# Norm products on maxima over four tokens, scalings and sums of the first layer moved between engines, and later reads of the raw weights

## The chip, the cores and the metric

The kernel runs on one core of a Trainium2 chip. A core has a matrix engine (TensorE, in the profile PE, with its weight loads as PEld), a vector engine (VectorE, DVE), a scalar engine (ScalarE, ACT), a general engine (GpSimd, POOL) and a queue engine (SyncE, SP). The engines run their own instruction streams and wait for each other through semaphores. SP and POOL issue most of the DMAs, each in its own order. The metric is the device time of one execution in microseconds (us).

## The reference

Two identical layers run over a sequence of 2048 tokens of width 448. Each layer is attention with 16 heads of 28 features, and then a gated unit of width 1792, both on normalised input and added to the residual:

```
x = x + A(_layernorm(x), wqkv, wo)
x = x + B(_layernorm(x), w_gate, w_up, w_down)
# twice, with the same weights

A:  scores = q @ k.T * Dh ** -0.5;  p = softmax(scores);  o = (p @ v) @ wo
B:  h = sigmoid(x @ w_gate) * (x @ w_up);  h @ w_down
```

All inputs and the output are float32.

## The kernel before

**Precision.** Float32 products are made of float16 matmuls: an operand is scaled by a power of two and split into a high and a low half, and three products (high by high, high by low, low by high) are summed in PSUM. The powers of two come from sums of squares of the weights, so each weight matrix is read once raw and measured before it can be split. The class `Measure` does that for a part of the later weights (`wo`, `w_down`, the first columns of `w_gate` and `w_up`) during the projection of layer 0: `read` loads one raw tile (`wo` and three of the four tiles of `w_down` on SP's queue, the rest on POOL's), `add` sums its squares into a column of `sums`, on DVE (L958), and for the second half of the gate and up tile on ACT (L965). The class `Prepare` does the rest during the attention.

**The projection.** The 2048 tokens are four blocks of 512, each of four tiles of 128. `project` works in this order: query and key products of block 0, values of block 0, the same of block 1, then the query and key products of blocks 2 and 3, then the values of both. `qk(b, ...)` makes seven tiles of 128 features by 512 tokens, each of eleven matmuls (L564), into four PSUM banks that go round (`evac[0] % 4`, shared with the value products). After each tile ACT writes the high half (L756), DVE the low half (L757), ACT the squares (L759), DVE the maximum of the two halves of the tokens (L761), and SP writes the halves to `qk_scr` in DRAM (L764). Then the entry of the list `fill` that belongs to the tile is called: work for other blocks is put there, and so stands at that place in every engine's stream. `vals(b, ...)` makes four tiles of values (L586 to L591); its entries of `after` stand ahead of the tile's evacuation on ACT (L793).

**Norm products.** The squares, after the maximum, are multiplied by an indicator of heads (`norm_products`, L735 and L738): four matmuls for the queries and four for the keys of a block, three tiles behind. Their maxima over the columns (L775) give the largest norm of a query and of a key for each head, with which a bound on every score is formed (`guard_of_norms`). The bound is subtracted ahead of the exponential; if it is above `GUARD_LIMIT / 2`, a slow branch finds the true maxima (`worst_of_heads`, `true_maxima`).

**A block's operands.** A later block is normalised and turned so that features lie on partitions. `norm` takes mean and variance on DVE (L287, L288) and the reciprocal root on POOL (L291, L293). Block 1 of layer 0 is scaled (`scale`, L320) and turned by PE into banks 6 and 7, two feature groups at a time (`turned`, L508); ACT and DVE split it from there. The other blocks go through DRAM: scaled and transposed in squares of 32 by DVE (`squares`, L337), stored by four DMAs (`store`, L349), gathered by two (`gather`, L357, L359), and split by ACT and DVE (`ready`, L218, L219). In the gated part of the kernel another form of the same step is in use: `norm_two` adds two POOL operations for an offset (L302, L304), `lift` scales on ACT (L308), `square` transposes on DVE (L316).

**Order.** The schedule is written by hand: each engine runs its instructions in the order in which the program names them. Buffers come from two pools of slots (`big` and `qrt`), in which the slot that has been free longest is given out first.

Of the kernel before, what the change touches and what calls it, by code (L numbers as in the profile page):

```python
# [42 lines left out]
UNIT = 32768.0  # L43
VC = 32
SLACK = 1.0201
GUARD_LIMIT = 56.0


POWER_OF_2 = (1.0000001192092896, -0.6931469440460205, 0.24022120237350464,
# [69 lines left out]
def interleaved_layers(ctx: ExitStack, tc: tile.TileContext, x_in, wqkv, wo, w_gate, w_up,  # L119
# [143 lines left out]
    class Block:  # L263
# [52 lines left out]
            nc.vector.transpose(self.xs[:, :, j, :], v)  # L316
            qrt.put(v)

        def scale(self, j):
            nc.vector.tensor_scalar(self.xn[:, j, :], x[:, self.b * TB + j, :],  # L320
                                    self.mv[:, j, 0:1], self.rs[:, j:j + 1],
                                    op0=ALU.subtract, op1=ALU.mult)

        def parts(self):
            self.all = big.get("xhl", [P, 7, W], F16)
# [274 lines left out]
    class WeightsQKV:  # L600
# [111 lines left out]
    def project(layer, wq, begun):  # L712
# [12 lines left out]
        def qk(b, blk, fill, before):  # L725
            pn = [bank(4 + 2 * (b % 2), "qnorm"), bank(5 + 2 * (b % 2), "knorm")]
            late = deque()

            def rows_of_heads(i):

                return ind[:, i:i + P // H, :].rearrange("p a h -> p (a h)")

            def norm_products(i, sq):
                if i <= 3:
                    nc.tensor.matmul(pn[0][:, 0:W // 2], rows_of_heads(i), sq[:, 0:W // 2],  # L735
                                     start=(i == 0), stop=(i == 3))
                if i >= 3:
                    nc.tensor.matmul(pn[1][:, 0:W // 2], rows_of_heads(1 + i), sq[:, 0:W // 2],  # L738
                                     start=(i == 3), stop=(i == 6))
                qrt.put(sq)  # L740

            for i in range(7):
                pm = bank(evac[0] % 4, "qkp")
                evac[0] += 1
                c = slice(i * P, (i + 1) * P)
                by_features(pm, blk, lambda kt: wq.qk[0][:, kt, c],
                            lambda kt: wq.qk[1][:, kt, c], i if layer == 0 and b == 0 else None)
                if layer == 0 and b == 0:
                    along[i]()
                if before and i in (1, 2):  # L750
                    before(i == 2)
                if len(late) == 3:
                    late.popleft()()
                hl = qrt.get("qkhl", [P, 2, W], F16)
                sq = qrt.get("sq", [P, W], BF16)
                nc.scalar.activation(hl[:, 0, :], pm, AF.Copy, scale=PS)  # L756
                nc.vector.scalar_tensor_tensor(hl[:, 1, :], pm, PS, hl[:, 0, :], op0=ALU.mult,  # L757
                                               op1=ALU.subtract)
                nc.scalar.activation(sq, hl[:, 0, :], AF.Square)  # L759

                nc.vector.tensor_tensor(sq[:, 0:W // 2], sq[:, 0:W // 2], sq[:, W // 2:W],  # L761
                                        op=ALU.max)
                n = slice(b * W, (b + 1) * W)
                nc.sync.dma_start(qk_scr[c, :, n], hl)  # L764
                qrt.put(hl)
                late.append(lambda i=i, sq=sq: norm_products(i, sq))
                if i < len(fill) and fill[i]:
                    fill[i]()

            def finish(whole=True):  # L770

                while len(late) > (0 if whole else 1):
                    late.popleft()()
                for i in range(2 if whole else 0):
                    nc.vector.tensor_reduce(peaks[:, i, b:b + 1], pn[i][0:H, 0:W // 2], axis=AX.X,  # L775
                                            op=ALU.max)
            return finish

# [42 lines left out]
        sq = lambda b, *js: lambda: blks[b].squares(js)  # L821
        b1, b2, b3 = blks[1:]
        if layer == 0:
            def scaled():
                b1.xn = big.get("xn", [P, TB, D])
                for j in range(TB):
                    b1.scale(j)

            def turned(kts):
                b1.turn_banks(6, kts)  # L830
                for j in range(TB):
                    b1.turn(j)
                b1.turned_high()
                b1.turned_low()

            fill = [idle, idle, lambda: b1.norm([0, 1]), lambda: b1.norm([2, 3]), idle, scaled]
            tell = Measure()
            along_values = {0: lambda: (b1.parts(), turned([0, 1]), tell.read(2)),
                            1: lambda: (turned([2, 3]), big.put(b1.xn), tell.read(2)),
                            2: lambda: (fin(), b2.norm(), tell.read()),  # L840
                            3: lambda: (b2.squares(), b2.store(), tell.read())}
        else:
            ones_of_values()
            fill = [idle, lambda: b1.ready(0, 1), lambda: b1.ready(2, 3), b2.norm,
                    lambda: b2.squares([0, 1]), sq(2, 2, 3), b2.store]
            along_values = {0: b3.norm, 1: sq(3, 0, 1), 2: lambda: (fin(), b2.gather()),
                            3: sq(3, 2, 3)}
        fin = qk(0, blks[0], fill, None)
        vals(0, blks[0], along_values)
        if layer == 0:  # L850
            fill = [b2.gather, b3.norm, sq(3, 0, 1), sq(3, 2, 3), idle,
                    lambda: b2.ready(0, 1), lambda: (b2.ready(2, 3), b3.store())]
        else:
            fill = [idle, lambda: b2.ready(0, 1), lambda: b2.ready(2, 3), b3.store]
        fin = qk(1, b1, fill, None)
        vals(1, b1, {0: b3.gather, 2 if layer == 0 else 1: fin})
        add = tell.add if layer == 0 else idle
        fin = qk(2, b2, [idle, lambda: b3.ready(0, 1), lambda: b3.ready(2, 3), idle, add, add,
                         add], None)
        fin = qk(3, blks[3], [add, add, add], fin)  # L860
        if layer > 0:
            big.put(*wq.qk)
# [62 lines left out]
    class Measure:  # L925
# [27 lines left out]
        def add(self):  # L953
            kind, t, n = self.rows.popleft()
            m, n = {"o": (3, n), "d": (6, n), "gu": (4, 1024)}[kind]
            v = t[:, 0:n]
            junk = big.get("junk", [P, 2048], BF16)
            nc.vector.tensor_tensor_reduce(junk[:, 0:n], v, v, 1.0, sums[:, m:m + 1],  # L958
                                           op0=ALU.mult, op1=ALU.add,
                                           accum_out=self.part[:, 0:1])  # L960
# [945 lines left out]
```

## Time and profile before

| | |
|---|---|
| runs shown | 1895.25 us median of 3 (1894.69 to 1895.59) |
| profiled execution, first to last instruction (span) | 1893.0 us |
| median of the runs less that span | 2.25 us |
| projection of layer 0, from the first product to the first scores | 13.0 to 118.4 us |
| projection of layer 1 | 953.5 to 1055.3 us |
| granted TensorE clock | 1.000 |

The page gives the profiled execution by its span; what lies around it is seen only as the difference to the runs. The rows that follow are of three kinds. A row of the timeline has the start in us, the duration in us, the engine, the line of the kernel, the operation, the tiles (out, then in), the shape and the number of instructions merged; what ended the engine's idle time ahead of it stands in brackets. A row of the groups has the count, then the busy time in us and the mean of one in ns, then the idle time ahead. A row of the waits has who waited for whom, the total in us, how often, and the longest.

### The profile page before, as it was taken

Reading aid. Unit: us, or ns where it says so; the run is one execution under the profiler, and the core shown is the slowest. Engines: PE = TensorE matmul, PEld = TensorE weight load, DVE = VectorE, ACT = ScalarE, POOL = GpSimd, SP = SyncE. Lnnn points to the kernel's source line nnn. Section 1 sums busy time; section 2 is a strip of 40 time slices with the busy share of each in tenths; the row PEclk is TensorE's granted clock in tenths of the full one; section 3 lists DMA queues with packets and bytes.
Section 4 is the critical chain, followed back from the end, with each engine's and each line's share of the span. In section 5 each row is a group of like instructions: output and inputs, shape, how many; then the busy total and the mean of one; then the engine's idle time right before and its main releaser. Section 6 shows DMA issues by size and latency. Waiting matters only on the chain. (4 is left out here: it accounts for less than half of the span.)

```text
span 1893.0 us, 56282 instructions
## 1 busy us (share of the span) xinstructions
PE 1886.5 (100%) x24254; PEld 1323.1 (70%) x24254; DVE 1430.7 (76%) x2835; ACT 1382.7 (73%) x1772; POOL 231.5 (12%) x453
## 2 busy tenths in 40 slices
PE   9999999999999999999999999999999999999999
PEld 4455555555556799999954556667666567999998
DVE  7758989898976688787564487787778676887664
ACT  5569999999993566555345799999999745565541
POOL 3023112222101111111100000000000020121110
PEclk9999999999999999999999999999999999999999
DMA  7676454334323566646734322122120245666553
GB/s 247 194 212 166 132 137 128 107 119 129 103 88 121 192 205 235 231 181 238 251 96 134 90 52 47 32 52 52 31 48 24 67 160 174 218 251 223 208 208 142
DMA packets 110882, 270.86 MB, mean 143 GB/s; under 512 B 13214, under 2 KB 67838, under 8 KB 110496
## 3 DMA queue, kind: packets, MB, share of 16 engines
q0 software_dynamic: 31776, 158.51, 23.4%
q1 hardware_dynamic: 78288, 108.20, 20.3%
q8 instruction: 192, 3.15, 0.7%
q10 hardware_dynamic: 560, 0.46, 0.1%
q14 instruction: 66, 0.54, 0.1%
HBM read 207.88 MB, written 50.85 MB: 137 GB/s over the span
## 5 line engine op out<-in xcount | busy, mean ns | idle before, releaser
L1222 ACT ACTIVATE prob_s<-sc 128x1536 f32<-128x1536 f32 (+1 forms) x657 | 887.9, 1487 | 6.6 <-PE sc L1207 5.9
L1258 PE MATMUL acc<-prob_s,val_s 128*32 128x256 f32 (+3 forms) x7700 | 569.9, 383 | 0.0
L1207 PE MATMUL sc<-qp_s 114*32 114x512 f16 x7868 | 553.2, 379 | 0.0
L579 PEld LDWEIGHTS <-gu_s 128*128 128x128 f16 x4368 | 426.9, 98 | 46.8 <-issue 0.4
L1207 PEld LDWEIGHTS <-qp_s 114*32 114x32 f16 x8192 | 272.7, 95 | 203.4 <-issue 88.3
L1258 PEld LDWEIGHTS acc<-prob_s,val_s 128*32 128x32 f32 x7700 | 272.3, 110 | 142.9 <-issue 13.6
L579 PE MATMUL chain<-xwide_s,gu_s 128*128 128x256 f16 x2016 | 247.5, 273 | 0.0
L1552 PE MATMUL dnp<-dn_s,hparts_s 128*128 128x224 f16 x2016 | 225.2, 259 | 0.0
L1552 PEld LDWEIGHTS <-hparts_s 128*128 128x128 f16 x2016 | 194.0, 98 | 4.4
L1238 DVE SCALAR_TENSOR_TENSOR power_q<-power_q,expo_q 128x512 f32<-128x512 f32 x243 | 168.2, 692 | 8.3
L1625 ACT COPY one_q<-chain 128x256 f32<-128x256 f32 x224 | 82.4, 371 | 121.4 <-PE chain L579 120.8
L1641 DVE TENSOR_TENSOR one_q<-side,one_q 128x512 f32<-128x512 f32 x112 | 72.2, 686 | 101.8 <-PE side L579 101.5
L579 PE MATMUL side<-xshort_s,gu_s 128*128 128x256 f16 x1120 | 140.5, 273 | 0.0
L564 PE MATMUL qkp<-xhl_s,wqk_s 128*128 128x512 f16 x616 | 138.1, 379 | 0.7 <-ACT wqk_s L231 0.2
L564 PEld LDWEIGHTS <-wqk_s 128*128 128x128 f16 x616 | 60.1, 98 | 69.8 <-ACT wqk_s L231 1.1
L1437 POOL DMA_DIRECT2D gu_s<-gu_parts x104 | 56.0, 538 | 430.5 <-PE side L579 424.5
L1287 DVE STREAM_TRANSPOSE oturned_q<-acc 128x512 f32<-128x512 f32 x32 | 22.9, 716 | 97.1 <-PE acc L1258 96.9
L1258 PE MATMUL acc<-power_q,val_s 128*32 128x256 f32 (+3 forms) x300 | 94.2, 396 | 0.0
L579 PE MATMUL side<-xwide_s,gu_s 128*128 128x256 f16 x672 | 91.6, 273 | 0.0
L1505 ACT CAST hparts_s<-hsums_q 128x256 f16<-128x256 f32 (+1 forms) x136 | 65.0, 494 | 30.2 <-DVE hsums_q L1517 20.2
L756 ACT ACTIVATE qkhl_q<-qkp 128x512 f16<-128x512 f32 x56 | 33.2, 593 | 71.9 <-PE qkp L564 68.3
L1652 ACT ACTIVATE one_q<-one_q 128x512 f32<-128x512 f32 x56 | 35.2, 629 | 64.3 <-DVE one_q L1641 64.3
(218 smaller groups left out, 2318.0 us busy)
## 6 DMA issues: line engine op xcount, KB each, us to landing
gu_s<-gu_parts POOLq DMA_DIRECT2D x104, 800.0 KB, 6.0
dn_s<-dn_parts POOLq DMA_DIRECT2D x42, 784.0 KB, 7.8
qp_s<-qk_scr SPq DMA_DIRECT2D x96, 224.0 KB
qk_scr<-qkhl_q SPq DMA_DIRECT2D x56, 256.0 KB
gu_parts<-pack_s POOLq DMA_DIRECT2D x14, 800.0 KB, 3.8
xt_scr<-xs_s SPq DMA_DIRECT2D x48, 224.0 KB
xraw_s<-xt_scr SPq DMA_DIRECT2D x12, 768.0 KB
qp_s<-qk_scr SPq DMA_DIRECT2D x64, 112.0 KB
```

The source lines that it names most:

```text
L564: nc.tensor.matmul(pm, w, x, start=(i == 0), stop=(i == len(terms) - 1))
L579: nc.tensor.matmul(pm, a, x, start=(first and i == 0), stop=(i == len(terms) - 1), skip_group_check=True)
L1207: nc.tensor.matmul(ps[32 * j:32 * j + 32, :], hd.k[:, keys], hd.q[:, qb * W:(qb + 1) * W], start=True, stop=True, tile_position=(0, 32 * j))
L1222: nc.scalar.activation(prob[:, 0:n, :], ps[:, 0:n, :], AF.Exp, scale=exp_scale)
L1238: nc.vector.scalar_tensor_tensor(p, p, c[k], y, op0=ALU.add, op1=ALU.mult)
L1258: nc.tensor.matmul(acc[qb * VC:(qb + 1) * VC, s], v[:, kc % TB, h, :], probs[c * NB + qb][:, s], start=(kc == 0 and a == 0), stop=(kc == N ...
L1437: queue.dma_start(self.gu[-1][m], gu_parts[p, m])
L1505: nc.scalar.copy(to[:, :, 0], a)
L1552: nc.tensor.matmul(pm, a[:, x, t], w[:, p, y], start=(begin and n == 0 and (j == 0 or alone)), stop=(n == 2), skip_group_check=True)
L1625: nc.scalar.copy(to, pm)
L1641: nc.vector.tensor_tensor(one[m], side[m], one[m], op=ALU.add)
L1652: nc.scalar.activation(out, v, AF.Sigmoid, scale=gate_scale)
```

## The change

- The maximum over two tokens is followed by a second one over the halves of its result, so that each column stands for four tokens. The norm products and the reductions behind them take 128 columns instead of 256, in both layers. `GUARD_LIMIT` goes from 56 to 72.
- Layer 0, block 1: tiles 0 and 1 are scaled on POOL, right after their statistics and ahead of those of tiles 2 and 3 in POOL's order; tiles 2 and 3 on DVE, where all four were.
- Layer 0, blocks 2 and 3: `norm_two`, `lift` and `square` take the place of `norm` and `squares`, so the scaling is ACT's. Block 2's gather moves from the entry of block 1's first tile to the second, where block 3's statistics stay, and block 3's store moves from the seventh tile to the fourth.
- The six raw tiles are read one at a time from block 1's third tile to block 2's third tile; they were read along block 0's values.
- The first and third tile of `w_down` are squared and summed on ACT, with a small addition on DVE, instead of on DVE.

```diff
-GUARD_LIMIT = 56.0
+GUARD_LIMIT = 72.0
...
-        def scale(self, j):
-            nc.vector.tensor_scalar(self.xn[:, j, :], x[:, self.b * TB + j, :],
-                                    self.mv[:, j, 0:1], self.rs[:, j:j + 1],
-                                    op0=ALU.subtract, op1=ALU.mult)
+        def scale(self, j, engine=nc.vector):
+            engine.tensor_scalar(self.xn[:, j, :], x[:, self.b * TB + j, :],
+                                 self.mv[:, j, 0:1], self.rs[:, j:j + 1],
+                                 op0=ALU.subtract, op1=ALU.mult)
...
-                    nc.tensor.matmul(pn[0][:, 0:W // 2], rows_of_heads(i), sq[:, 0:W // 2],
+                    nc.tensor.matmul(pn[0][:, 0:P], rows_of_heads(i), sq[:, 0:P],
                                      start=(i == 0), stop=(i == 3))
...
-                nc.vector.tensor_tensor(sq[:, 0:W // 2], sq[:, 0:W // 2], sq[:, W // 2:W],
-                                        op=ALU.max)
+                for n in (W // 2, P):
+                    nc.vector.tensor_tensor(sq[:, 0:n], sq[:, 0:n], sq[:, n:2 * n], op=ALU.max)
...
-                    nc.vector.tensor_reduce(peaks[:, i, b:b + 1], pn[i][0:H, 0:W // 2], axis=AX.X,
+                    nc.vector.tensor_reduce(peaks[:, i, b:b + 1], pn[i][0:H, 0:P], axis=AX.X,
                                             op=ALU.max)
...
+            def both_norms(blk):
+                blk.norm_two(0)
+                blk.norm_two(2)
+
+            def lifted(blk, *js):
+                for j in js:
+                    blk.lift(j)
+                    blk.square(j)
+
+            def scaled_aside():
+                b1.xn = big.get("xn", [P, TB, D])
+                for j in (0, 1):
+                    b1.scale(j, nc.gpsimd)
+
             def scaled():
-                b1.xn = big.get("xn", [P, TB, D])
-                for j in range(TB):
+                for j in (2, 3):
                     b1.scale(j)
...
-            fill = [idle, idle, lambda: b1.norm([0, 1]), lambda: b1.norm([2, 3]), idle, scaled]
+            fill = [idle, idle, lambda: (b1.norm([0, 1]), scaled_aside()),
+                    lambda: b1.norm([2, 3]), idle, scaled]
             tell = Measure()
-            along_values = {0: lambda: (b1.parts(), turned([0, 1]), tell.read(2)),
-                            1: lambda: (turned([2, 3]), big.put(b1.xn), tell.read(2)),
-                            2: lambda: (fin(), b2.norm(), tell.read()),
-                            3: lambda: (b2.squares(), b2.store(), tell.read())}
+            along_values = {0: lambda: (b1.parts(), turned([0, 1])),
+                            1: lambda: (turned([2, 3]), big.put(b1.xn)),
+                            2: lambda: (fin(), both_norms(b2)),
+                            3: lambda: (lifted(b2, 0, 1, 2, 3), b2.store())}
...
-            fill = [b2.gather, b3.norm, sq(3, 0, 1), sq(3, 2, 3), idle,
-                    lambda: b2.ready(0, 1), lambda: (b2.ready(2, 3), b3.store())]
+            fill = [idle, lambda: (b2.gather(), both_norms(b3)),
+                    lambda: (lifted(b3, 0, 1), tell.read()),
+                    lambda: (lifted(b3, 2, 3), b3.store()), tell.read,
+                    lambda: (b2.ready(0, 1), tell.read()), lambda: b2.ready(2, 3)]
...
-        vals(1, b1, {0: b3.gather, 2 if layer == 0 else 1: fin})
+        vals(1, b1, {0: lambda: (b3.gather(), layer or tell.read()), 2 if layer == 0 else 1: fin})
         add = tell.add if layer == 0 else idle
-        fin = qk(2, b2, [idle, lambda: b3.ready(0, 1), lambda: b3.ready(2, 3), idle, add, add,
-                         add], None)
+        read = tell.read if layer == 0 else idle
+        fin = qk(2, b2, [read, lambda: b3.ready(0, 1), lambda: (b3.ready(2, 3), read and read()),
+                         idle, add, add, add], None)
...
+            if kind == "d" and len(self.rows) % 2 == 0:
+                nc.scalar.activation(junk[:, 0:n], v, AF.Square, accum_out=self.part[:, 1:2])
+                big.put_next(junk)
+                nc.vector.tensor_tensor(sums[:, m:m + 1], sums[:, m:m + 1], self.part[:, 1:2],
+                                        op=ALU.add)
+                big.put(t)
+                return
```

More of the change, by code (lines that the diff above doesn't have):

```diff
@@ L734, in norm_products @@
                 if i <= 3:
-                    nc.tensor.matmul(pn[0][:, 0:W // 2], rows_of_heads(i), sq[:, 0:W // 2],
+                    nc.tensor.matmul(pn[0][:, 0:P], rows_of_heads(i), sq[:, 0:P],
                                      start=(i == 0), stop=(i == 3))
                 if i >= 3:
-                    nc.tensor.matmul(pn[1][:, 0:W // 2], rows_of_heads(1 + i), sq[:, 0:W // 2],
+                    nc.tensor.matmul(pn[1][:, 0:P], rows_of_heads(1 + i), sq[:, 0:P],
                                      start=(i == 3), stop=(i == 6))
```

## The prediction

> **What bounds the kernel now.** I read the page's busy shares first, then the waits of TensorE (PE), then the timelines of the engines in the two projections, since the diff touches nothing else.
>
> ```profile
> span 1893.0 us, 56282 instructions
> PE 1886.5 (100%) x24254; PEld 1323.1 (70%) x24254; DVE 1430.7 (76%) x2835; ACT 1382.7 (73%) x1772; POOL 231.5 (12%) x453
> PE still L261 <- DVE warm L179: 1.3, 1, 1.3
> PE turn L508 <- DVE xn_s L320: 0.8, 1, 0.8
> ...
> ```
>
> PE is busy all the time, but a busy PE need not be at its peak. The list of PE's waits for other engines, over the whole run, has two more rows of 0.2 us: 2.5 us in all, every one ahead of 16 us, in the start-up. What it does afterwards is read from the pitch, start to start:
>
> ```profile
> 28.70 0.27 PE L735 MATMUL qnorm<-sq_q,ind 128*128 128x256 bf16 x1
> 28.81 2.54 PE L564 MATMUL qkp<-xhl_s,wqk_s 128*128 128x512 f16 x11
> 31.18 0.27 PE L735 MATMUL qnorm<-sq_q,ind 128*128 128x256 bf16 x1
> 924.77 28.91 PE L1552 MATMUL dnp<-dn_s,hparts_s 128*128 128x224 f16 x300
> ```
>
> Eleven matmuls of 512 columns take 31.18 - 28.81 = 2.37 us, 215 ns each; 256 columns take 110 (28.70 to 28.81); 300 of 224 take 28.91 less the last one's 0.26, 95.5 each. That is one line, 0.417 ns a column and 2 ns. The projections of both layers run on it without a break, so PE sets their length, and work taken from VectorE (DVE) is worth only what PE waits for DVE.
>
> **The change, part by part.**
>
> *Norm products (64 matmuls, 256 to 128 columns).*
>
> ```profile
> L735 PE MATMUL qnorm<-sq_q,ind 128*128 128x256 bf16 x32 | 8.7, 272 | 0.0
> L738 PE MATMUL knorm<-sq_q,ind 128*128 128x256 bf16 x32 | 6.4, 273 | 0.0
> L735 PEld LDWEIGHTS <-ind 128*128 128x128 bf16 x32 | 3.2, 100 | 3.7
> L638 PEld LDWEIGHTS sums<-sums,ones 128*128 128x128 f32 x4 | 0.8, 190 | 0.3
> 18.40 0.28 PE L638 MATMUL sums<-sums,ones 128*128 128x1 f32 x2
> 18.54 0.59 PE L564 MATMUL qkp<-xhl_s,wqk_s 128*128 128x512 f16 x2
> ```
>
> All 64 stand in the dense stretches, so each saves its pitch. No row has 128 columns behind full weights of 16 bits. The line gives 55 ns. The nearest short matmuls are the sums: one moving column, full float32 weights, 0.14 us for two, 70 ns. Their weight load is recorded at 190 ns, a norm product's at 100, so the new pitch should lie under 70. The other end is 110, no gain, if the load of the next weights (98 ns in most rows) can't pass the shorter matmul; against that, the 224-column row keeps 95.5 with loads of 98. I take 60: 64 x (110 - 60) = 3.2 us, ends 0 and 64 x 55 = 3.5 us. The Trainium skill, "TensorE: Matmul & The Clock Gate", section "Back-to-back issue gap", gives about 81 ns for 128 columns in a stream of loads and matmuls, by which the saving would be 1.9 us; its 131 ns for 512 columns is not what this trace shows (215).
>
> *The second maximum on DVE (56 more) and shorter reductions (16).*
>
> ```profile
> 24.59 0.28 DVE L761 TENSOR_TENSOR sq_q<-sq_q 128x256 bf16<-128x256 bf16 x1
> 24.79 0.62 DVE L287 BATCH_NORM_STATS2 st<-x 128x6 f32<-128x448 f32 x1
> 60.97 0.65 DVE L757 SCALAR_TENSOR_TENSOR qkhl_q<-qkp,qkhl_q 128x512 f16<-128x512 f32 x1
> 61.67 0.35 PE L589 MATMUL vp<-wv_s,xhl_s 128*128 128x448 f16 x1
> 99.01 0.67 DVE L757 SCALAR_TENSOR_TENSOR qkhl_q<-qkp,qkhl_q 128x512 f16<-128x512 f32 x1
> 100.31 2.54 PE L564 MATMUL qkp<-xhl_s,wqk_s 128*128 128x512 f16 x11
> 975.07 0.27 DVE L761 TENSOR_TENSOR sq_q<-sq_q 128x256 bf16<-128x256 bf16 x1
> 976.93 0.49 PE L738 MATMUL knorm<-sq_q,ind 128*128 128x256 bf16 x3
> ```
>
> One maximum over 256 holds DVE for 0.20 us; over 128 it is between 0.10 and 0.20, I take 0.15: 8.4 us of DVE, nothing on PE while DVE keeps ahead of the banks. Four PSUM banks go round, so a PE group waits for the evacuation of the fourth one before it. The tightest places are these three. Block 1: DVE ends at 61.62, PE takes the bank at 61.67. Block 3: 99.68 against 100.31. Layer 1: the squares are ready at 975.34, PE wants them at 976.93; five maxima since DVE's last slack (0.75 us) fit in 1.6 us. The first two would break by seven and eleven maxima (1.05 and 1.65 us) if the rest of the change gave nothing back; it does, next.
>
> *Scalings of blocks 2 and 3 to ScalarE (ACT).*
>
> ```profile
> L308 ACT ACTIVATE lifted_q<-x,off,rs 128x448 f32<-128x448 f32 x32 | 22.7, 754 | 0.0
> 603.40 0.19 POOL L291 TENSOR_SCALAR rs<-mv 128x2 f32<-128x2 f32 x1 [18.13 <-DVE mv L288]
> 605.07 0.19 POOL L291 TENSOR_SCALAR rs<-mv 128x2 f32<-128x2 f32 x1
> 43.71 0.18 DVE L288 BATCH_NORM_AGGREGATE mv<-st 128x2 f32<-128x6 f32 x1
> 42.43 9.66 PE L564 MATMUL qkp<-xhl_s,wqk_s 128*128 128x512 f16 x44
> ```
>
> Eight scalings, 0.45 us each by the four at 32.87 below, leave DVE between 45 and 61 us: 3.6 us against 1.05 us of maxima, so block 1's tight place gains about 2.5 us. ACT gets eight lifts of 0.75. POOL gets four operations for each pair of tiles, 1.67 us a pair (603.40 to 605.07, same code). The new wait: in block 0 the lifts stand ahead of the evacuation of value tile 3, and behind ACT's wait all of block 1's evacuations are queued. Block 2's statistics end at 43.9 as they do now, POOL's second pair at 45.7 (1.67 later, 0.1 for handing over), the last two lifts at 47.2 (two at 0.75; the first two are done by then), the evacuation, half a lift longer or less, at 47.8. PE needs that bank at the fourth tile of block 1, 42.43 + 3 x 2.37 = 49.5: 1.7 us spare. At block 1's third tile ACT waits for POOL again: block 3's statistics begin on DVE at about 50.5, two tiles take 1.5, POOL's pair 1.7, two lifts 1.5, so the fourth tile's evacuation starts on ACT at 55.2 and ends on DVE at about 56.5; its bank is wanted at 59.6 (61.67 less a value tile of 2.1). Both cost nothing.
>
> *Block 1's scaling, two tiles on POOL.*
>
> ```profile
> 10.70 0.29 POOL L200 CAST ind<-ind_f_q 128x128 bf16<-128x128 f32 x1
> 26.72 0.72 POOL L293 TENSOR_TENSOR rs<-rs,nhalf 128x2 f32<-128x2 f32 x1
> 32.87 1.78 DVE L320 TENSOR_SCALAR xn_s<-x,mv,rs 128x448 f32<-128x448 f32 x4
> 33.48 1.66 PE L508 MATMUL turn<-ident,xn_s 128*128 128x128 f32 x8
> 34.98 0.35 PE L589 MATMUL vp<-wv_s,xhl_s 128*128 128x448 f16 x1
> 37.07 1.04 PE L508 MATMUL turn<-ident,xn_s 128*128 128x128 f32 x8
> 37.94 0.35 PE L589 MATMUL vp<-wv_s,xhl_s 128*128 128x448 f16 x1
> ```
>
> By the cast (0.29 us for 128 elements) a tile of 448 takes up to 1.0 us on POOL, and no less than DVE's 0.5: from 27.5 the two end by 29.5, and tiles 2 and 3's reciprocal roots, now behind them, about 1 us later, wanted at 33.5. The first eight transposes take 1.50 us, the next eight 0.87: 0.63 us in which PE follows DVE's scalings tile by tile (a wait of the weight loads, so the list above doesn't have it). Two scalings fewer (0.9 us) against five maxima (0.75 us) bring DVE about level, though the first two tiles wait no longer. Ends 0 and 0.6 us; I take 0.2, the smaller half, since the second eight need banks that DVE frees just ahead of 37.07.
>
> *Reads, adds, stores and gathers.*
>
> ```profile
> 37.71 1.80 SPq L949 DMA_DIRECT2D raw_s<-in_B_w_down_dram  x3
> 73.73 0.38 SPq L357 DMA_DIRECT2D xraw_s<-xt_scr  x1
> 79.20 1.14 ACT L218 CAST xhl_s<-xraw_s 128x512 f16<-128x512 f32 x2 [4.75 <-DMA xraw_s<-xt_scr]
> 106.37 0.55 POOL L881 TENSOR_TENSOR bnd<-bnd,half 16x1 f32<-16x1 f32 x1 [50.58 <-DVE bnd L879]
> 85.08 2.08 DVE L958 CUSTOM_DVE_ANT_0 junk_s<-raw_s,sums 128x1792 bf16<-128x1792 f32 x1
> 15.08 1.69 ACT L633 ACTIVATE junk_s<-wraw_s 128x1792 bf16<-128x1792 f32 x1
> ```
>
> Three loads of wo and three of w_down (0.6 us of SP's queue each) move behind block 1's qk_scr writes; the seven of POOL's queue move into the 50.6 us in which POOL idles. Block 3's four stores go three tiles (7 us) ahead in SP's queue, past three qk_scr writes and two of the reads, which take some 3 us of that back; so its gather, issued at 73.73 and needed at 79.20 now, lands near 75. Block 2's gather waits one write longer, but its stores come about 2 us sooner, since four scalings (1.8 us) stand no longer between the transposes. Each raw tile has ten or more us before its sum. Two sums of 2.08 us go to ACT at 1.69 and a short read of the sum; DVE then waits for ACT instead of working, about as long, but starts from 4 us less lag. Cost nothing; without that lead block 3's 0.63 us would go first.
>
> Sum: 3.2 + 0.2 = 3.4 us, the span at 1889.6. The runs shown have a median of 1895.25, 2.25 us above this span; the same around it gives 1891.9. The attention follows PE and starts that much sooner. The raised limit matters only if the slow branch were taken: the bound on these inputs, worked out from the reference, grows from 19.3 to 23.7 over both layers, against 28 and now 36.
>
> **The rivals.**
>
> *The weight load holds the pitch.* If the short matmul can't hide the next load, the pitch lies between the sums' 70 and the load's 98: a saving of 2.6 to 0.8 us, 1892.7 to 1894.5, the transposes left out. For it speaks that each load starts with the matmul ahead of it; against it, the loads of 98 at a pitch of 95.5. Chance 0.2. The skill's 81 ns would put it at 1893.4.
>
> *More than forecast.* The line holds (3.5 us) and the transposes lose their whole 0.6: 4.1 us, 1891.2. Nothing in the trace forbids it but the bank at 37.07. Chance 0.2.
>
> *Slower: the lifts make PE wait.* If POOL's eight operations ahead of the lifts take longer, ACT is late for block 1's fourth tile. It decides from 1.7 us of delay, and the gain is lost at 1.7 + 3.4 = 5.1. POOL at twice its time (3.3 us more) gives a wait of 1.6, 1893.5; at three times, 4.9, and again as much at block 1's third tile less its 3 us spare, 1898.7. For it: three engines hand over in turn, with all evacuations behind. Against it: the same chain ran in 1.67 us beside a working DVE. The Trainium skill, "SBUF — State Buffer", section "SBUF: two separate sides", speaks against the change here: DVE and GpSimd share a port pair, held for a whole instruction. No row here shows POOL held up by it. Chance 0.1, half of that above the old time.
>
> **How the numbers follow.** The forecast has 0.5. A measurement of this kernel tells 0.2% (3.8 us) from no change, so faster means below 1891.5: all of the second rival, and a tenth where the forecast's own spread (1891.4 to 1892.7) crosses: 0.3. Slower, above 1899, keeps 0.05. Same 0.65. The range 1890.8 to 1895.4 holds forecast and two rivals with the runs' spread of 0.5 us.
>
> **What would show it.** Norm products at 55 to 65 ns from the next start; no PE wait between 20 and 105 us; value tile 3 of block 0 evacuated near 47.8 on ACT; block 3's cast near 75 without a DMA wait; the first score matmuls 1.8 us sooner in layer 0 and 3.4 in layer 1. A pitch near 98, or a PE wait for an evacuation in block 1, makes the prediction wrong.

## The result and the profile after

The changed kernel takes 1898.04 us (median of 21 runs, 1897.19 to 1898.86) against 1895.20 for the kernel before on the same chip: a ratio of 1.0013, 95% interval 1.0007 to 1.0019. The forecast was 1891.9 with a range of 1890.8 to 1895.4. The change costs 2.8 us where a gain of 3.4 was forecast. The page's first lines and the list of TensorE's (PE's) waits, in the form of those of before:

```profile
span 1896.2 us, 56361 instructions
PE 1884.9 (99%) x24254; PEld 1343.2 (71%) x24254; DVE 1432.9 (76%) x2877; ACT 1390.6 (73%) x1784; POOL 239.0 (13%) x467
PE vp L589 <- DVE qkhl_q L757: 2.5, 1, 2.5
PE turn L508 <- DVE xn_s L320: 1.7, 1, 1.7
PE still L261 <- DVE warm L179: 1.3, 1, 1.3
PE knorm L738 <- DVE sq_q L762: 0.5, 1, 0.5
PE vp L590 <- DVE wv_s L234: 0.4, 1, 0.4
...
```

There was no wait after 16 us; now there are three of 0.4 us or more, the longest of 2.5 us (the rows of the transposes and of L261 belong to the start-up, as before). To place the loss I matched the starts of all 24254 matmuls of two profiles one by one in program order, each counted from its own first query and key product (that product starts anywhere from 12.5 to 15.4 us, depending on the loads). The differences of those starts, summed by stage of the kernel before, are used all through this document (us; plus is a loss). The last column is the difference of the medians of the runs. It isn't the sum of the others: the start-up varies, and outside the two projections, where the edits change no instruction, the starts drift by up to 0.6 us, which I didn't follow.

| kernel | 13.0 to 42.4 | 42.4 to 59.6 | 59.6 to 68.2 | 68.2 to 85.4 | 85.4 to 118.4 | layer 0, sum | layer 1 | whole, medians |
|---|---|---|---|---|---|---|---|---|
| after | +0.04 | -0.27 | **+4.15** | -0.27 | +0.11 | +3.77 | -1.71 | +2.84 |
| norm products alone | +0.62 | +0.10 | +0.38 | -0.27 | **+2.37** | +3.20 | -1.71 | +2.15 |
| after, old norm products | -0.60 | 0.00 | **+2.62** | +1.15 | 0.00 | +3.16 | 0.00 | +3.49 |
| after, lifts' own slot | +0.03 | -0.27 | -0.16 | **+5.73** | -0.59 | +4.75 | -1.71 | +1.06 |
| after, POOL's reads on SP | +0.03 | -0.27 | -0.10 | +0.63 | +0.58 | +0.87 | -1.71 | -0.92 |
| after, early reads | +0.03 | -0.27 | **+1.75** | -0.27 | -0.59 | +0.66 | -1.71 | -0.08 |
| late reads alone | +0.01 | 0.00 | +0.20 | **+10.63** | 0.00 | +10.83 | 0.00 | +10.13 |
| norm products, layer 1 only | 0.00 | 0.00 | +0.01 | 0.00 | 0.00 | 0.00 | -1.70 | -1.86 |
| norm products, second step on POOL | -0.06 | +0.15 | +0.12 | -0.21 | +0.85 | +0.86 | -1.55 | -1.14 |
| after, early reads and own slot | +0.03 | -0.27 | -0.01 | -0.27 | -0.59 | -1.10 | -1.71 | -2.19 |
| the same, second step on POOL | +0.47 | -0.27 | -0.16 | -0.27 | -0.50 | -0.71 | -1.55 | -3.30 |
| the same, block 1 scaled on VectorE | -0.05 | -0.27 | +0.22 | -0.27 | -0.50 | -0.86 | -1.55 | -3.28 |

The first row says most of it. The stages without a new wait are shorter by just what the norm products save, and layer 1, where the change consists of them alone, gains 1.71 us. One stage, the end of block 1, loses 4.15. It is read along the chain, from PE back. PE's timeline there, with a norm product from earlier on:

```profile
23.48 0.22 PE L735 MATMUL qnorm<-sq_q,ind 128*128 128x128 bf16 x1
23.54 0.60 PE L564 MATMUL qkp<-xhl_s,wqk_s 128*128 128x512 f16 x2
...
63.53 0.35 PE L587 MATMUL vp<-wv_s,xhl_s 128*128 128x448 f16 x1
66.36 0.35 PE L589 MATMUL vp<-wv_s,xhl_s 128*128 128x448 f16 x1 [2.47 <-DVE qkhl_q L757]
...
67.31 0.58 PE L590 MATMUL vp<-wv_s,xhl_s 128*128 128x448 f16 x1
67.68 0.58 PE L591 MATMUL vp<-wv_s,xhl_s 128*128 128x448 f16 x1
```

The gap from 63.53 to 66.36 is 2.64 us longer than the usual pitch of 0.19, and shortly after it the value products start 0.37 us apart instead of 0.19. The windows say why (us; then busy time and count of PE, its weight loads, DVE, ACT, POOL; granted clock, share of the DMA engines, GB/s):

```profile
64.00:66.00 2.00, 0.00 (x0) 0.00 (x0) 0.39 (x1) 0.99 (x2) 0.00 (x0) 1.00 1.02 280
66.00:68.00 2.00, 1.64 (x6) 0.74 (x6) 1.97 (x6) 1.97 (x5) 0.00 (x0) 0.72 1.09 267
68.00:70.00 2.00, 2.00 (x7) 0.84 (x6) 1.93 (x6) 2.00 (x5) 0.00 (x0) 0.50 1.09 324
70.00:72.00 2.00, 2.00 (x14) 1.18 (x13) 0.93 (x3) 0.74 (x2) 0.00 (x0) 0.92 1.14 354
```

After the pause the clock is at half for about 3.4 us, eight matmuls of 0.18 us more each, another 1.5 us in the profiled run. Eleven of the 21 runs have a granted clock of 1.000, more than 3.4 us at half would leave (0.9991), and yet a median of 1898.10, against 1898.0 of the other ten. So, as far as these runs show, the half clock adds nothing in the end; a likely reason, not tested by itself, is that a PE that comes earlier only waits longer for block 3's operands, which are late too, as shown below. The pause itself comes from ACT, whose timeline around it reads:

```profile
47.22 0.52 ACT L793 ACTIVATE val_s<-vp 128x448 f32<-128x448 f32 x1
...
55.09 0.57 ACT L756 ACTIVATE qkhl_q<-qkp 128x512 f16<-128x512 f32 x1
...
64.98 0.60 ACT L756 ACTIVATE qkhl_q<-qkp 128x512 f16<-128x512 f32 x1 [6.21 <-DMA qk_scr<-qkhl_q]
...
83.15 1.14 ACT L218 CAST xhl_s<-xraw_s 128x512 f16<-128x512 f32 x2 [4.58 <-DMA xraw_s<-xt_scr]
```

ACT stands 6.21 us ahead of the evacuation of block 1's sixth tile, not for PE but for a write of an earlier tile to DRAM to land: it needs that tile's slot. The slots of `qrt` (12) are given out in the order in which they came free. Followed through the program, the two halves of the sixth tile got the slot of an old tile of squares in the kernel before; the eight lifts take slots of the same pool, and now it gets the slot of the third tile of its own block. That tile's write is the second row below (SP's queue), issued at 56.02; ACT goes on at 64.98, so it took some 9 us to land. What surrounds it, on SP and then on POOL:

```profile
55.48 0.49 SPq L359 DMA_DIRECT2D xraw_s<-xt_scr  x1
56.02 0.60 SPq L764 DMA_DIRECT2D qk_scr<-qkhl_q  x1
56.66 0.69 SPq L211 DMA_DIRECT2D raw_s<-in_A_wo_dram  x1
...
59.34 7.70 SPq L349 DMA_DIRECT2D xt_scr<-xs_s  x4
```

```profile
55.48 0.86 POOL L966 DMA_DIRECT2D raw_s<-in_B_w_down_dram  x1
56.35 0.78 POOL L211 DMA_DIRECT2D raw_s<-in_B_w_gate_dram  x1
...
59.49 0.52 POOL L214 DMA_DIRECT2D raw_s<-in_B_w_up_dram  x1
```

POOL's seven reads are named in the entries of block 2, behind 68 us, but nothing on POOL holds them: they run right after its last statistics, at 55.48, a microsecond ahead of SP's reads of `wo` (56.66). From 58 us the DMA engines are full, as the stage windows of after show (59.6 to 68.2 against 0.91 before; 68.2 to 85.4 against 0.51):

```profile
59.60:68.20 8.60, 6.13 (x32) 2.99 (x29) 2.55 (x6) 3.16 (x6) 0.41 (x1) 0.92 1.04 305
68.20:85.40 17.20, 17.20 (x82) 8.02 (x81) 6.62 (x16) 7.76 (x16) 0.00 (x0) 0.94 1.06 356
```

Block 3's four stores take 7.70 us to issue instead of 3.43. Two smaller rows close the list, a pair of maxima on DVE and the scaling on POOL (the last from the groups: count, busy us, mean ns):

```profile
48.91 0.55 DVE L762 TENSOR_TENSOR sq_q<-sq_q 128x256 bf16<-128x256 bf16 x2
49.40 0.69 DVE L757 SCALAR_TENSOR_TENSOR qkhl_q<-qkp,qkhl_q 128x512 f16<-128x512 f32 x1
```

```profile
L320 POOL TENSOR_SCALAR xn_s<-x,mv,rs 128x448 f32<-128x448 f32 x2 | 3.8, 1882 | 0.1
```

The pair takes 0.49 us of DVE against 0.20 for the single maximum, and 0.46 in the median of all pairs, so the second costs 0.26 to 0.29, not 0.15. A tile costs POOL 1.9 us, not at most 1.0.

### The profile page after: what moved, and what is told of

The parts are those of the page before. It is cut to its first block, busy times and chain, and to the rows that moved or that the text cites. A ratio compares the mean times of both kernels' runs of the same rounds, so it can differ in the third digit from the quotient of the medians.

```text
span 1896.2 us, 56361 instructions
## 1 busy us (share of the span) xinstructions
PE 1884.9 (99%) x24254; PEld 1343.2 (71%) x24254; DVE 1432.9 (76%) x2877; ACT 1390.6 (73%) x1784; POOL 239.0 (13%) x467
## 5 line engine op out<-in xcount | busy, mean ns | idle before, releaser
L1231 PEld LDWEIGHTS <-qp_s 114*32 114x32 f16 x8192 | 284.3, 96 | 193.2 <-issue 83.1
L1282 PEld LDWEIGHTS acc<-prob_s,val_s 128*32 128x32 f32 x7700 | 284.8, 110 | 130.2 <-issue 12.3
```

The source lines that it names most:

```text
L1231: nc.tensor.matmul(ps[32 * j:32 * j + 32, :], hd.k[:, keys], hd.q[:, qb * W:(qb + 1) * W], start=True, stop=True, tile_position=(0, 32 * j))
L1282: nc.tensor.matmul(acc[qb * VC:(qb + 1) * VC, s], v[:, kc % TB, h, :], probs[c * NB + qb][:, s], start=(kc == 0 and a == 0), stop=(kc == N ...
```

## The experiments

The theory after this reading had two causes, the slots and the crowded DMA engines, with the dearer maxima as a third. All kernels compute the whole output; in the three with a POOL step, the second step adds the two values where the change takes the larger, so the bound is looser: worked out from the reference 30.7 on these inputs, under the changed limit's 36.

**Norm products alone.** The kernel before with nothing but the new norm products and second maxima.

```diff
-                nc.vector.tensor_tensor(sq[:, 0:W // 2], sq[:, 0:W // 2], sq[:, W // 2:W],
-                                        op=ALU.max)
+                for n in (W // 2, P):
+                    nc.vector.tensor_tensor(sq[:, 0:n], sq[:, 0:n], sq[:, n:2 * n], op=ALU.max)
```

> The kernel before with the norm products alone: maxima over four tokens, 128 columns, shorter reductions; scalings, reads and sums as before. The changed kernel's loss stands in block 1 of layer 0, where ScalarE waits 6.2 us for a slot and PE then waits 2.5 us. Theory A (that wait is made by the moved scalings and reads): this kernel has no such wait and keeps the saving of 64 x 54 ns = 3.5 us less what the second maxima cost at DVE's two tightest places (0.05 and 0.63 us spare, 1.05 and 1.65 us of maxima): 2.0 us of new waits at most, 1891.7 to 1893.7. Theory B (the second maxima overload DVE): a loss in block 1 as in the changed kernel, about 1896 or more.

Measured: 1897.31 us, ratio 1.0012 (1.0003 to 1.0021). The weight loads' waits have a row that is new:

```profile
PEld L735 <- DVE sq_q L762: 3.9, 5, 1.2
```

Five weight loads of norm products wait for DVE's maxima, three of them from 95 to 102 us, where DVE also sums the raw weights: DVE is full there (7.79 of 8 us busy from 95 to 103), and each 0.27 us more comes out at PE. The time is that of theory B, but the place is another: the end of block 1 loses only 0.38. So the maxima don't fit into layer 0 by themselves; the sharing out of DVE's work is not an extra, it pays for them.

**After with the old norm products.** The rest of the change alone, one maximum and 256 columns.

```diff
-                for n in (W // 2, P):
-                    nc.vector.tensor_tensor(sq[:, 0:n], sq[:, 0:n], sq[:, n:2 * n], op=ALU.max)
+                nc.vector.tensor_tensor(sq[:, 0:W // 2], sq[:, 0:W // 2], sq[:, W // 2:W],
+                                        op=ALU.max)
```

> The changed kernel with the norm products back at 256 columns and one maximum. Theory A: the wait of ScalarE for a slot and PE's wait of about 2.5 us stay, and the 3.5 us are lost on top: 1898.0 + 3.5 = 1901.5. Theory B: the waits go with the second maxima, and the time is about that of the kernel before, 1895.

Measured: 1898.65 us, 1.0018 (1.0009 to 1.0027). ACT's wait is there with the same length:

```profile
63.74 0.60 ACT L756 ACTIVATE qkhl_q<-qkp 128x512 f16<-128x512 f32 x1 [6.32 <-DMA qk_scr<-qkhl_q]
```

PE pauses 2.35 us for it, and 1.15 more at 84 us for block 3's operands; no half clock follows. So the large loss doesn't come from the norm products. The time lies between the two theories, 2.9 us under theory A's. The first stage gains 0.60 us: with DVE less loaded, the two scalings on POOL do give the transposes their whole upper end.

**The lifts in a slot of their own.** After, with all four lifts of a block in one slot of `big`, so that they leave `qrt`'s turn as it was.

```diff
-            self.lifted[j] = qrt.get("lifted", [P, D])
+            if j == 0:
+                self.lifts = big.get("lifts", [P, TB, D])
+            self.lifted[j] = self.lifts[:, j, :]
```

> The changed kernel with the eight lifted tiles of blocks 2 and 3 in a large slot of their own, so that the ring of small slots turns as slowly as before; the order of every engine and all DMAs stay. Slot theory (tile 6 of block 1 gets the slot of tile 3, whose write to qk_scr has not landed, because eight lifts have used up the free slots in between): ScalarE's wait of 6.2 us is gone, and with it PE's 2.5 us and the half clock after it (1.6 us): 1898.0 - 4.1 = 1893.9. Crowding theory (the transfers are late in themselves, and block 2's gather, next in ScalarE's order, lands as late as tile 3's write): the wait moves to the gather and most of the loss stays, 1897 to 1898.

Measured: 1896.22 us, 1.0006 (0.9997 to 1.0015). ACT's wait for the slot is gone, and with it the loss of that stage (-0.16). It comes back later: block 3's gather is issued at 72.84 and lands 10 us after, and the PE row is that of the norm products (L771 is the second maximum here, nine lines further down than in after):

```profile
82.90 1.14 ACT L218 CAST xhl_s<-xraw_s 128x512 f16<-128x512 f32 x2 [9.39 <-DMA xraw_s<-xt_scr]
```

```profile
PE qnorm L744 <- DVE sq_q L771: 4.1, 1, 4.1
```

In after the same cast starts at 83.15, but PE is 4 us later by then and does not notice. So both theories of this run hold in part: the slot's wait is the lifts' doing, and the transfers are late in themselves. The profiled execution is one of the longer ones of this kernel (1897.28 us), and eight matmuls at half clock behind the wait are in its 5.73 us (1.7), so they overstate the median.

**POOL's reads on SP.** After, with the fourth tile of `w_down` and the gate and up tile read from SP's queue, which does keep them in place.

```diff
-                queue = nc.sync if kind == "o" or j < 3 and kind == "d" else nc.gpsimd
+                queue = nc.sync
```

> The changed kernel with the last tile of w_down and the gate and up tile read through SP's queue, so that they can't start ahead of their place; POOL's queue started them at 55.5 us, two tiles into block 1. Crowding theory: tile 3's write lands sooner, ScalarE's wait shrinks from 6.2 us to 2 or less, PE doesn't wait: about 1894. Slot theory alone: the slot is still that of tile 3, whose write stands behind block 2's gather and in front of wo in SP's queue; the wait shrinks only by what the POOL reads held it up: 1895 to 1898.

Measured: 1894.24 us, 0.9995 (0.9986 to 1.0004). ACT's wait is halved (the forecast had 2 us or less), and PE no longer feels it:

```profile
62.53 0.60 ACT L756 ACTIVATE qkhl_q<-qkp 128x512 f16<-128x512 f32 x1 [2.98 <-DMA qk_scr<-qkhl_q]
...
81.00 1.14 ACT L218 CAST xhl_s<-xraw_s 128x512 f16<-128x512 f32 x2 [5.91 <-DMA xraw_s<-xt_scr]
```

That queue alone decides 3.8 us. Block 3's gather is still late (0.63 us at PE).

**Early reads.** After, with all six raw tiles read along block 0's values as before.

```diff
-            along_values = {0: lambda: (b1.parts(), turned([0, 1])),
-                            1: lambda: (turned([2, 3]), big.put(b1.xn)),
+            along_values = {0: lambda: (b1.parts(), turned([0, 1]), tell.read(2)),
+                            1: lambda: (turned([2, 3]), big.put(b1.xn), tell.read(2)),
...
```

> The changed kernel with the six raw tiles read where the kernel before reads them, along block 0's values; lifts, POOL's scalings, ScalarE's sums and the norm products as changed. Reads theory (the late reads crowd the queues in which block 2's and 3's stores, gathers and the writes to qk_scr stand; slots only pass the delay on): no wait of ScalarE for a slot of more than 1 us, block 3's operands by 78 us, PE loses nothing between 59 and 85 us: 4.1 us less than the changed kernel, 1894, of which about 1.5 us of waits for the norm products' squares and for the values' weights remain. Slot theory: the lifts still shorten the ring, tile 6 still waits for tile 3's write, at least 2 us of PE are lost in block 1: 1896 or more.

Measured: 1895.10 us, 0.9999 (0.9990 to 1.0008). Block 3's stage now has its saving, but the slot's wait remains, in ACT's list of waits from 40 to 120 us:

```profile
ACT qkhl_q L756 <- DMA qk_scr<-qkhl_q: 4.7, 2, 4.4
```

So the slots lose time without any late read: 1.75 us at PE in the profile. Neither theory is right alone: the wait is longer than the 1 us of the first, the loss smaller than the 2 us of the second.

**Late reads alone.** The kernel before, with only the reads where the change puts them.

```diff
-            along_values = {0: lambda: (b1.parts(), turned([0, 1]), tell.read(2)),
+            along_values = {0: lambda: (b1.parts(), turned([0, 1])),
...
-            fill = [b2.gather, b3.norm, sq(3, 0, 1), sq(3, 2, 3), idle,
-                    lambda: b2.ready(0, 1), lambda: (b2.ready(2, 3), b3.store())]
+            fill = [b2.gather, b3.norm, lambda: (b3.squares((0, 1)), tell.read()),
+                    sq(3, 2, 3), tell.read, lambda: (b2.ready(0, 1), tell.read()),
+                    lambda: (b2.ready(2, 3), b3.store())]
...
```

> The kernel before with the later reads alone, in the places where the changed kernel has them. Reads theory: block 3's gather, needed within 1.1 us of its landing in the kernel before, lands several us later, ScalarE stands before its cast and PE waits in block 2, 2 to 5 us with the half clock behind: 1897 to 1900. If late reads do harm only together with the lifts' hold on the slots: within 0.5 us of the kernel before, 1895.

Measured: 1905.31 us, 1.0053 (1.0040 to 1.0067). Here block 3's stores stand at the seventh tile, behind the reads, and the wait that the lifts' own slot showed is half as long again:

```profile
ACT xhl_s L218 <- DMA xraw_s<-xt_scr: 18.0, 2, 13.9
```

So the reads lose time without any lift, and more than in after and than either forecast: PE stands 8.4 us more in block 2 and then runs ten matmuls at half clock. The stores are issued by 78.0 here and by 67.0 in after, so the change's earlier store of block 3 seems to take back part of what its reads cost; no run has that store alone.

**Norm products in layer 1 only.** One maximum and 256 columns in layer 0, the new form in layer 1, on the kernel before.

```diff
+            n = P if layer else W // 2
...
+                for m in (W // 2, P)[:1 + layer]:
+                    nc.vector.tensor_tensor(sq[:, 0:m], sq[:, 0:m], sq[:, m:2 * m], op=ALU.max)
```

> The kernel before with the maxima over four tokens in layer 1 alone. In all kernels with the shorter norm products layer 1's projection is 1.71 us shorter, without a wait: 32 x 53.4 ns. Expected 1895.2 - 1.7 = 1893.5, whichever theory holds of layer 0.

Measured: 1893.32 us, 0.9990 (0.9981 to 0.9999), layer 0 unchanged to 0.01 us and layer 1 shorter by 1.70, 32 products at 53 ns less each. A few lines of code get half of what was forecast for the whole change.

**The second step on POOL.** The norm products alone, but DVE's second maximum replaced by an addition on POOL.

```diff
+                nc.gpsimd.tensor_tensor(sq[:, 0:P], sq[:, 0:P], sq[:, P:2 * P], op=ALU.add)
```

> The kernel before with the shorter norm products, where the second step over the tokens is a sum on POOL instead of a second maximum on DVE (still a bound on the norm, a larger one). DVE theory (alone, the second maxima cost DVE 0.27 us each and so about 5 us of PE waits in layer 0): the waits in block 3 go, 3.5 us are kept less a wait for POOL at the last tile of a block: 1891.7 to 1893. If DVE's load isn't the cause of the waits, they stay: 1896 to 1897.5.

Measured: 1894.04 us, 0.9992 (0.9983 to 1.0001). Against the form on DVE, layer 0 loses 0.86 us instead of 3.20, both after the norm products' saving. That is more than the forecast of 1891.7 to 1893 allowed. What is left is PE's wait for POOL, whose addition takes up to 2.2 us beside DVE's sums of raw weights (see the last section); behind two of these additions PE loses 0.58 us each:

```profile
PE qnorm L735 <- POOL sq_q L763: 0.7, 2, 0.4
```

**Early reads and the lifts' own slot.** Both causes removed from after: the edits of these two experiments together.

```diff
+            b2.own_lifts = b3.own_lifts = True
...
+            along_values = {0: lambda: (b1.parts(), turned([0, 1]), tell.read(2)),
+                            1: lambda: (turned([2, 3]), big.put(b1.xn), tell.read(2)),
...
```

> The changed kernel with both repairs: reads in the places of the kernel before, and the lifted tiles in a large slot of their own. Two-cause theory (each repair alone left the other cause: early reads kept ScalarE's wait for the slot, 4.4 us, with 1.75 us lost in block 1; own lifts kept the late gather, 5.7 us lost in block 2): no PE wait between 40 and 100 us; layer 0's projection 1.2 us shorter than in the kernel before, layer 1's 1.7: 1892.3. If a third cause, such as DVE's load with the second maxima, is what binds once these are gone: the waits move to the norm products in block 3, 1893.5 to 1895.

Measured: 1893.07 us, 0.9991 (0.9982 to 1.0000). The losses between 59.6 and 85.4 are gone, and no wait of PE of more than 0.2 us is left between 40 and 100, as the theory of two causes said; the largest loss left is 0.55 us near 31 us, where PE waits for the split of `wv` on DVE. The time lies between the two forecasts, 0.8 us over the first. Block 3's cast starts with hardly a wait, where the prediction had it:

```profile
74.60 1.14 ACT L218 CAST xhl_s<-xraw_s 128x512 f16<-128x512 f32 x2 [0.20 <-DMA xraw_s<-xt_scr]
```

This is the test of the two causes together: 5.0 us between it and after, while either cure alone leaves 3.2 (own slot) and 2.0 (early reads).

**The same with the second step on POOL.**

```diff
-                for n in (W // 2, P):
-                    nc.vector.tensor_tensor(sq[:, 0:n], sq[:, 0:n], sq[:, n:2 * n], op=ALU.max)
+                nc.vector.tensor_tensor(sq[:, 0:W // 2], sq[:, 0:W // 2], sq[:, W // 2:W],
+                                        op=ALU.max)
+                nc.gpsimd.tensor_tensor(sq[:, 0:P], sq[:, 0:P], sq[:, P:2 * P], op=ALU.add)
```

> The last one with the second step over the tokens as a sum on POOL, a larger bound. DVE theory: the wait for the values' weights at the end of block 0 (0.55 us) goes, and the other waits stay away: about 1891.7. Against it: POOL's sum takes 0.6 us and stands behind the scalings of block 1 (1.9 us each) and the offsets on POOL, so a norm product may wait for POOL: up to 1893.5.

Measured: 1891.96 us, 0.9985 (0.9976 to 0.9994), better than both kernels. One wait is left: POOL's addition for a tile of block 0 stands behind POOL's two scalings (L772 is the addition here), and it takes 1.17 us itself instead of the usual 0.42. Of the 3.30 us against the kernel before, 0.58 lie in the attention. That drift is no merit of this edit: late reads alone show it too (0.54 by 560 us).

```profile
32.39 0.22 PE L744 MATMUL qnorm<-sq_q,ind 128*128 128x128 bf16 x1 [1.32 <-POOL sq_q L772]
```

```profile
27.39 3.82 POOL L329 TENSOR_SCALAR xn_s<-x,mv,rs 128x448 f32<-128x448 f32 x2
31.17 1.17 POOL L772 TENSOR_TENSOR sq_q<-sq_q 128x128 bf16<-128x128 bf16 x1
```

**And block 1's scalings on VectorE again.**

```diff
-            fill = [idle, idle, lambda: (b1.norm([0, 1]), scaled_aside()),
+            fill = [idle, idle, lambda: b1.norm([0, 1]),
...
-                for j in (2, 3):
+                for j in range(TB):
```

> Edit: the kernel with early reads, lifts in a slot of their own and the second step as a POOL addition, and in it block 1's four scalings all on VectorE again (POOL scales nothing of block 1). The theory that the last wait left in that kernel, 1.3 us of PE's norm product for POOL's addition near 30.7 us, comes from POOL's two scalings of 1.9 us each ahead of that addition: the wait goes, and with it the stretch from 13 to 33 us loses about 1.3 us; VectorE's 0.9 us for two more scalings stands ahead of the transposes, whose wait grows from 1.2 towards 1.7 at most. 1890.7 to 1891.3 us, a ratio of about 0.998 to the kernel before. The rival, that POOL's addition is late for another cause (its own 0.42 us behind VectorE's maximum): the wait stays over 1 us and the time stays at 1892.0 or rises by the scalings' 0.9 us to 1892.9.

Measured: 1891.71 us, 0.9982 (0.9973 to 0.9991). The wait at 30.7 us went as the theory said, from 1.3 us to nothing, and the stretch from 13.0 to 33.4 lost 1.30 us. But the time moved by only 0.25 us, and against its own runs of the kernel before not at all (-3.28 after -3.30): the transposes follow DVE's scalings again and give 0.78 back by 42.4, and 0.38 more goes at the end of block 1. The forecast time here was missed because the wait removed had covered the next one.

## Why the prediction was wrong

**Norm products: right, and a little more.** The row at 23.48 has the next start 0.06 us on, and layer 1's 1.71 us over 32 products are 53 ns each. So the new pitch is about 56, where the line said 55 and 60 was taken; the whole saving is 3.4 us, near the upper end. The rival of the weight load fell. So, on this trace, did the Trainium skill's 81 ns ("TensorE: Matmul & The Clock Gate", "Back-to-back issue gap").

**The second maximum: mis-sized.** "I take 0.15" between 0.10 and 0.20; it takes 0.26 to 0.29, outside the bound. The bound assumed that half the columns can't cost more than the whole ones. "Nothing on PE while DVE keeps ahead" failed in layer 0: 4.9 us of waits when nothing is shared out (the 3.20 of the table and the 1.71 that the products save there), and still 0.64 in after at 109 us.

**Lifts on ACT: the chain was right, "Both cost nothing" was not.** Value tile 3 was evacuated at 47.22 to 47.74 (47.8 forecast) and block 1's fourth tile at 55.09 (55.2). The step counted engines and banks and left out that a lift needs a slot. The wait came two tiles after the place named in the rival, and POOL's chain, the rival's mechanism, was on time; that a PE wait in block 1 stood among the signs of being wrong was right, its cause was not foreseen.

**Scalings on POOL.** 1.9 us a tile was outside the bounds too, taken from a cast of 128 columns. The transposes' 0.6 us appears in full when the maxima stay away (-0.60); in after 0.15 of it remains (34.02 to 35.37, 1.35 us for the first eight instead of 1.50), close to the 0.2 that was taken.

**Reads, adds, stores and gathers: "Cost nothing" is the step that failed.** It put POOL's reads into POOL's idle time at the place where the program names them, though nothing on that queue waits there, and counted what SP's queue has to issue rather than when it lands. With the reads early (early reads and own slot) the gather is issued at 68.02 and does land near 75; in after it is issued at 73.47 and lands at 83, 9.7 us later. "Without that lead block 3's 0.63 us would go first" named the right place.

**The sum.** 3.4 us was forecast. The parts that were said to cost nothing, and the mis-sized maxima, cost PE some 5.3 us in the profile: 2.64 and 1.5 at the end of block 1, 0.55 near 31 us, 0.64 at 109; 0.5 more, outside the projections, is the drift whose cause I didn't follow. The norm products gave 1.71 in each layer, the transposes 0.15. The slower side had a chance of 0.05, for one mechanism that did not occur; that DMAs land later when their sources crowd was not among the rivals. That the time stayed within 3.8 us of the old one, which was given 0.65, is luck: it is the difference of a gain and a loss of which the second was not foreseen.

## What to carry to other kernels

A buffer taken from a shared ring shortens the turn for everything else in it, so before a step gets a buffer, find out whose write the next users will then wait for. A read that is moved to a later line of the program moves only as far as something on its own queue waits, and what it costs is when the others' transfers land. When an engine at its limit is given more, move the relief first and measure the dearer instruction by itself, since a smaller shape need not be cheaper.

## What was not expected of the hardware

**A pause of 2.8 us was followed by half the clock.** In after 2.83 us from start to start (2.47 idle) were followed by the half clock shown above. With the old norm products a pause of 2.54 us (2.19 idle) was not: the windows of that kernel, same columns as above, stay at 1.00.

```profile
64.00:66.00 2.00, 0.89 (x5) 0.48 (x5) 1.42 (x3) 1.97 (x5) 0.00 (x0) 1.00 1.07 274
66.00:68.00 2.00, 1.89 (x13) 1.00 (x11) 1.91 (x5) 1.97 (x5) 0.00 (x0) 1.00 1.07 306
```

The Trainium skill, "TensorE: Matmul & The Clock Gate", section 'Part 1: The HAM clock gate (the "warmup" mystery)', speaks of an idle window of about 3.4 us that runs freely. The trace's 2.47 us of idle time are shorter than that. Length alone doesn't decide: in the start-up of the run with early reads 2.12 us of idle time, less than the 2.19 above, were followed by half the clock (four transposes in 1.12 us, later in 0.60):

```profile
9.05 1.12 PE L508 MATMUL turn<-ident,xn_s 128*128 128x128 f32 x4 [2.12 <-DVE xn_s L320]
...
12.50 0.60 PE L508 MATMUL turn<-ident,xn_s 128*128 128x128 f32 x4
```

What does decide is open.

**POOL stands while DVE runs some instructions.** In the last kernel of the experiments the POOL addition usually takes 0.42 us. Beside DVE's sums of raw weights it ends 0.28 us after them, whatever their length; POOL first, then DVE:

```profile
84.90 0.42 POOL L772 TENSOR_TENSOR sq_q<-sq_q 128x128 bf16<-128x128 bf16 x1 [0.86 <-DVE sq_q L770]
87.16 2.20 POOL L772 TENSOR_TENSOR sq_q<-sq_q 128x128 bf16<-128x128 bf16 x1 [1.84 <-DVE sq_q L770]
...
92.52 1.27 POOL L772 TENSOR_TENSOR sq_q<-sq_q 128x128 bf16<-128x128 bf16 x1 [1.93 <-DVE sq_q L770]
95.02 1.34 POOL L772 TENSOR_TENSOR sq_q<-sq_q 128x128 bf16<-128x128 bf16 x1 [1.23 <-DVE sq_q L770]
```

```profile
87.00 2.08 DVE L989 CUSTOM_DVE_ANT_0 junk_s<-raw_s,sums 128x1792 bf16<-128x1792 f32 x1
...
92.36 1.15 DVE L989 CUSTOM_DVE_ANT_0 junk_s<-raw_s,sums 128x896 bf16<-128x896 f32 x1
...
94.81 1.27 DVE L989 CUSTOM_DVE_ANT_0 junk_s<-raw_s,sums 128x1024 bf16<-128x1024 f32 x1
```

The ends are 89.36 against 89.08, 93.79 against 93.51, 96.36 against 96.08. This agrees with the rule of the Trainium skill, "SBUF — State Buffer", section "SBUF: two separate sides", by which a pair of ports is held for a whole instruction. The prediction had said that no row showed POOL held up; the rows of before had no POOL work beside the sums of raw weights (POOL is idle from 55.8 to 106.4). In after POOL's reciprocal root at 32.21 took 1.51 us instead of 0.72 beside the split of `wv`, while the lifts' chain kept its forecast times. The other way round the trace of after doesn't show a hold for the whole instruction: during POOL's second scaling (29.89 to 31.77) a maximum on DVE took 0.68 us instead of 0.28 and ended at 30.75, and the split of `wv`, begun at 30.93, took its usual 1.15.
